# Four dense layers with their operands as scaled pairs of float16 instead of float32r, in longer phases

## The chip, the core and the metric

The kernel runs on one core of a Trainium2 chip. The metric is device time in microseconds (us) of one execution. Engines of the core that matter here: TensorE (PE in the profile, its weight loads PEld), VectorE (DVE), ScalarE (ACT), GpSimd (POOL) and SyncE (SP), which issues nearly all DMAs. Each engine works through its own queue in order.

## What is computed

An attention with a soft cap over 2 batches, 12 heads, 448 rows and 64 columns a head, then two dense pairs of layers on the 896 x 768 result:

```python
scores = cap * np.tanh(scale * np.matmul(q, k.transpose(0, 1, 3, 2)) / cap)
attn = softmax(scores)                     # sum + 1e-9 below the line
x = np.matmul(attn, v)                     # 896 tokens x 768
h = x @ w_in;  g = np.maximum(h, 0.0) ** 2 # 768 -> 2048
x = g @ w_out                              # 2048 -> 768
h = x @ w_in2; g = h / (1 + np.exp(-h))
out = g @ w_out2
```

The weights arrive as 64-bit floats; the kernel's own units turn them into 32-bit words first.

## The kernel before

**Attention** (`attention_bounded`, lines 413 to 583). Twelve pairs of heads (i = 0 to 11), two half steps each. For a half step PE makes the scores (L440), ACT takes tanh (L448) and exp (L451), DVE adds two exp tiles into a `half` tile (L469, L471), PE makes `px` = exp times v (L459) and, with a tile of ones, the row sums (L479). All these matmuls are in float32. DVE copies `px` into the cell `x_c{i}` (L490) and the sums into `sm` (L494); after every second pair the sums go through DRAM, where DVE inverts them (L508, L509) and a DMA spreads them into `rb` (L517). DVE multiplies the cell by `rb` (L522), and `Forms.now` lets POOL split the cell into a high part (L1031) and a low part (L1032) for the first dense layer. Cells 10 and 11 are divided without the detour (L529 to L531): their reciprocals are 128 x 448 and lie on DVE after everything else of the attention.

**Dense layers** a, b, c, d (`feed_forward`, lines 667 to 974). Every operand is split in two parts, high = the value in float32r, low = value minus high; a product is high*high + high*low + low*high, so three matmuls of K = 128. Weight tiles: ACT takes the head of the 64-bit float (L209), DVE shifts and joins it (L216) into the word `u`, ACT writes the high part (L237), DVE the low part (L248). Layers a and c work on pairs of inner tiles f, f+1 (2048 / 128 = 16 tiles): `Pair.plain` with 72 matmuls of 448 columns for (a,0), (a,2), (c,0), and else a scheme with seven products instead of eight, 63 matmuls, which needs sums and differences of the operands (`Pair.whole`, L262 and L1070 build them). The results are activated on ACT and split into `g` tiles (`parts`, L675). Layers b and d (`out_units`) multiply `g` with the second weights: 12 units of 448 columns (b) and 14 of 384 columns (d).

**Phases.** The 16 inner tiles go in four phases of four: two pairs of layer a, then the 12 units of b over these four tiles, and so on; after each phase but the first the new sums are added to `y` on DVE (L662) or written out by ACT. The same holds for c and d.

**Order.** All of it is laid out in Python before anything runs: `Stream` keeps a clock of its own for ACT, DVE and POOL with priced steps, and `chunk` puts background steps (weights, forms, splits) into the gaps in order of due time. PE's order is fixed by the program. Five weight slots `hl`, three raw tiles, four words `u`.

**End.** All engines load `cap` into a register after the first phase (L905); where its size is above 50 a second program (`attention_general` and the layers once more, names ending in g) runs after the first. In this case it doesn't.

In names of the profile a number of a buffer is left out: `ha_0f` is h of layer a, batch 0, for either tile of the pair; `x0f` holds the parts of the cells; a final f marks the first program.

## Time and profile before

| | |
|---|---|
| three runs | 549.84 us median, 549.43 to 553.88 |
| the profiled execution | 549.33 us |
| its span, first to last instruction | 547.4 us |
| PE busy | 539.6 us (99%) |
| DVE busy / ACT busy / POOL busy | 364.3 / 355.6 / 31.1 us |

The profiled execution is 1.9 us longer than its span. A busy PE is not PE at its peak, since matmuls overlap; pace is read from the time that a run of matmuls takes, divided by their number. "Idle before" in square brackets is the wait of that engine just before the instruction, with what ended it.

### The profile page before, as it was taken

The numbers are of one execution on the slowest core, as the hardware profiler recorded it, in microseconds if no ns is written. First come the engines' busy times: TensorE is split into PE (matmuls) and PEld (weight loads), VectorE is DVE, ScalarE is ACT, GpSimd is POOL, SyncE is SP. The second block draws the span as 40 slices with busy tenths as digits, with TensorE's granted clock in tenths as the row PEclk, the third lists the DMA queues.
The fourth block names the chain that finished last, engine by engine and source line by source line (L and its number), as shares of the span: only waits on it lengthen the run. The fifth ranks groups of instructions, "written<-read, shape, count | busy, mean of one in ns | idle before, by whom it ended". The sixth has DMA issues, their size and how long they took to land.

```text
span 547.4 us, 7123 instructions
## 1 busy us (share of the span) xinstructions
PE 539.6 (99%) x2739; PEld 452.6 (83%) x2739; DVE 364.3 (67%) x525; ACT 355.6 (65%) x533; POOL 31.1 (6%) x27
## 2 busy tenths in 40 slices
PE   8999999999999999999999999999999999999995
PEld 4333333899999999999999999999999999999995
DVE  0779987896755667566756997654686568656621
ACT  6999998388668626862688797756762486238400
POOL 1004444200000000000000000000000000000000
PEclk9999999999999999999999999999999999999999
DMA  8365552152331353135313331633351335130022
GB/s 224 128 178 163 171 180 85 58 186 103 116 116 59 115 174 115 59 116 173 116 59 115 116 116 58 223 124 116 116 174 59 115 113 176 59 115 1 23 108 77
DMA packets 18300, 64.25 MB, mean 117 GB/s; under 512 B 2578, under 2 KB 8722, under 8 KB 18258
## 3 DMA queue, kind: packets, MB, share of 16 engines
q1 hardware_dynamic: 18224, 63.72, 35.7%
q8 instruction: 23, 0.38, 0.3%
q14 instruction: 19, 0.16, 0.1%
q0 software_dynamic: 32, 0.00, 0.0%
q10 hardware_dynamic: 2, 0.00, 0.0%
HBM read 60.88 MB, written 2.79 MB: 116 GB/s over the span
## 4 chain that ended last, share of the span: by engine, by line
PE 97%; DMA 1%; SPq 0%; DVE 0%; issue 0%
PE px L459 7%; PE s L440 7%; PE yb_1f L686 4%; PE yb_4f L686 4%; PE yb_2f L686 4%; PE yb_0f L686 4%; PE yb_3f L686 4%; PE yb_5f L686 4%; PE yd_0f L956 3%; PE yd_6f L956 3%; PE yd_1f L956 3%; PE yd_3f L956 3%; PE yd_5f L956 3%; PE yd_4f L956 3%; PE yd_2f L956 3%; PE ha_0f L686 3%
## 5 line engine op out<-in xcount | busy, mean ns | idle before, releaser
L448 ACT ACTIVATE e<-s 112x896 f32<-112x896 f32 x48 | 41.7, 933 | 7.1 <-PE s L440 7.1
L451 ACT ACTIVATE e<-e 112x896 f32<-112x896 f32 x48 | 43.5, 975 | 0.0
L469 DVE TENSOR_TENSOR half<-e,e 112x896 f32<-112x896 f32 x24 | 27.4, 1147 | 2.9 <-ACT e L451 2.9
L471 DVE TENSOR_TENSOR half<-half,half 112x896 f32<-112x896 f32 x11 | 14.8, 1349 | 0.4
L494 DVE COPY sm<-sum 128x448 f32<-128x448 f32 x10 | 6.2, 621 | 8.8 <-PE sum L479 8.8
L479 PE MATMUL sum<-half,ones 112*64 112x448 f32 x52 | 11.9, 541 | 0.0
L662 DVE TENSOR_TENSOR x1f<-yaf,x1f 128x448 fp32r<-128x448 f32 x15 | 9.2, 621 | 1.4 <-ACT x1f L658 1.2
L662 DVE TENSOR_TENSOR ycf<-yd_6f,ycf 128x384 f32<-128x384 f32 x6 | 3.3, 558 | 9.1 <-PE yd_6f L956 9.1
L658 ACT ACTIVATE x1f<-yaf 128x448 fp32r<-128x448 f32 x15 | 8.4, 570 | 0.9 <-DVE yaf L662 0.8
L479 PEld LDWEIGHTS sum<-half,ones 112*64 112x64 f32 x52 | 3.6, 137 | 6.2 <-issue 4.9
L662 DVE TENSOR_TENSOR ycf<-yd_0f,ycf 128x384 f32<-128x384 f32 x6 | 3.3, 558 | 7.9 <-PE yd_0f L956 7.9
L662 DVE TENSOR_TENSOR yaf<-yaf 128x448 f32<-128x448 f32 x12 | 7.2, 622 | 0.5 <-ACT yaf L658 0.3
L662 DVE TENSOR_TENSOR ycf<-yd_5f,ycf 128x384 f32<-128x384 f32 x6 | 3.3, 558 | 5.7 <-PE yd_5f L956 5.7
L662 DVE TENSOR_TENSOR ycf<-yd_4f,ycf 128x384 f32<-128x384 f32 x6 | 3.3, 558 | 4.4 <-PE yd_4f L956 4.4
L662 DVE TENSOR_TENSOR ycf<-yd_1f,ycf 128x384 f32<-128x384 f32 x6 | 3.3, 558 | 4.2 <-PE yd_1f L956 4.1
L530 DVE RECIPROCAL r<-r 128x448 f32<-128x448 f32 x2 | 5.9, 2953 | 0.1
L237 ACT ACTIVATE hl_58f<-u_59f 128x768 fp32r<-128x768 f32 x1 | 0.8, 847 | 7.8 <-PE yd_6f L956 7.8
L237 ACT ACTIVATE hl_68f<-u_69f 128x768 fp32r<-128x768 f32 x1 | 0.8, 847 | 7.8 <-PE yd_6f L956 7.8
L209 ACT ACTIVATE zeros<-raw_wa9f 128x768 f16<-128x768 bf16 x1 | 1.1, 1087 | 7.1 <-DVE u_18f L216 7.1
L209 ACT ACTIVATE zeros<-raw_wa13f 128x768 f16<-128x768 bf16 x1 | 1.1, 1083 | 7.1 <-DVE u_28f L216 7.1
L662 DVE TENSOR_TENSOR ycf<-yd_3f,ycf 128x384 f32<-128x384 f32 x6 | 3.3, 558 | 3.4 <-PE yd_3f L956 3.3
L662 DVE TENSOR_TENSOR yaf<-yb_5f,yaf 128x448 f32<-128x448 f32 x4 | 2.5, 625 | 4.6 <-PE yb_5f L686 4.6
(2232 smaller groups left out, 1872.7 us busy)
## 6 DMA issues: line engine op xcount, KB each, us to landing
out<-ycf SPq DMA_DIRECT2D x14, 192.0 KB
rb<-scratch SPq DMA_DIRECT2D x10, 224.0 KB
raw_wb_0f<-in_moe_w_out SPq DMA_DIRECT2D x2, 768.0 KB
raw_wb_1f<-in_moe_w_out SPq DMA_DIRECT2D x2, 768.0 KB
raw_wb_2f<-in_moe_w_out SPq DMA_DIRECT2D x2, 768.0 KB
raw_wb_3f<-in_moe_w_out SPq DMA_DIRECT2D x2, 768.0 KB
raw_wb_4f<-in_moe_w_out SPq DMA_DIRECT2D x2, 768.0 KB
raw_wb_5f<-in_moe_w_out SPq DMA_DIRECT2D x2, 768.0 KB
```

The lines of the kernel that those rows point to most:

```text
L440: nc.tensor.matmul(sp[:CP, j, :S], lhsT=pr.qk[i][p, 1, c * CP : (c + 1) * CP], rhs=pr.qk[i][p, 0], start=True, stop=True,)
L448: nc.scalar.activation(t, sp[:CP, :, :S], AF.Tanh, scale=scale_s)
L451: nc.scalar.activation(ex[i, c], ex[i, c], AF.Exp, scale=scale_c)
L459: nc.tensor.matmul(px[i][64 * j : 64 * j + 64, :S], lhsT=pr.vt[i][:, j, c], rhs=ex[i, c][:, j], start=(c == 0), stop=(c == NC - 1),)
L469: nc.vector.tensor_tensor(t, ex[i, 2 * g], ex[i, 2 * g + 1], op=ALU.add)
L471: nc.vector.tensor_tensor(t, t, half[i, 0], op=ALU.add)
L479: nc.tensor.matmul(sums[i][64 * j : 64 * j + 64, :S], lhsT=ones[:CP], rhs=t[:, j], start=(n == 0), stop=(n == len(parts) - 1),)
L494: nc.vector.tensor_copy(t, sums.pop(i)[:, :S])
L658: return Step("A", cols, lambda: nc.scalar.activation(at(out), at(src), func), list(deps))
L662: return Step(eng, cols, lambda: e.tensor_tensor(at(out), at(x), at(y), op=op), list(deps))
L686: nc.tensor.matmul(acc, lhsT=w(e_w, kk), rhs=x(e_x, kk), start=first and i == 0, stop=last and i == len(n) - 1, skip_group_check=more,)
L956: nc.tensor.matmul(acc[:, :NW], lhsT=g[KD * e + kk][:, e_g, t * 128 : t * 128 + 128], rhs=hl[:, e_w, kk * NW : kk * NW + NW], start=first ...
```

## The change

The bounded program `f` gets its dense operands as float16 pairs: each operand is multiplied by a power of two (`POWER`) before it is split, and the results are scaled back in ACT's `scale` or in DVE's scalar operand. Tiles of the same bytes hold twice as many values, so there are ten weight slots instead of five. The general program keeps float32r and its four phases of four; both are written by the same code with another type and another plan.

In float16 PE gets a weight load and a matmul as two instructions for each product, where in float32r one instruction stands. The products are the same in number and shape: 1611 of 448 columns and 672 of 384 columns in the dense layers.

The phases of `f` are 4, 6 and 6 inner tiles in layers a and b, and 8 and 8 in c and d. The results of b are written once and added twice (before: three times), those of d written once and added once.

A watch is added: the low parts of all operands but the b weights and layer a's `g` are made with an accumulator output (`accum_out`, 144 instructions), 22 samples of high parts are squared and summed (`look` on DVE for cells 0 to 9, `sample` on ACT for twelve others), and at the end DVE judges them (`judge`), PE adds the 22 columns up over the partitions (L239 of the new kernel), and every engine loads the verdict `ok` (L1106) ten units into the last 14 units. The second program runs where `ok` is not 1.0; the register of `cap` is gone.

The planner looks six steps ahead in the background queues (`AHEAD`) instead of one, and may move a high part or a square from ACT to DVE (`either`). Counted in `f`: steps of 448 columns on DVE outside the attention 187 before, 202 now; sums of 384 columns 42 and 14; steps of 448 columns on ACT 265 and 246. DMAs carry the same bytes.

```diff
+    POWER = {"x0": 16, "a": 13, "b": 14, "ga": 22, "x1": 23, "c": 13, "d": 14, "gc": 24}
+    LOWS, SAMPLES = 224, NP2 + 10
+    LEAST = 256.0 * 128 * S
+    ONE = 2.0 ** -POWER["x0"]
...
+    COL2, COL4 = 0.1892, 0.1625
+    PROD, UNIT = 9 * COL2, 12 * COL2
...
+    plans = {"f": Plan((4,6,6),(8,8)), "g": Plan((4, 4, 4, 4), (4, 4, 4, 4))}
...
+    def low_part(watch, lo, x, hi, scale, see=True):
+        if watch is None:
+            nc.vector.tensor_tensor(lo, x, hi.bitcast(F32), op=ALU.subtract)
+        else:
+            nc.vector.scalar_tensor_tensor(
+                lo, x, scale, hi, op0=ALU.mult, op1=ALU.subtract, accum_out=watch.low() if see else None
+            )
...
+        def low(self):
+            self.n += 1
+            return self.lows[:, self.n - 1 : self.n]
...
+        def look(self, x):
+            self.m += 1
+            nc.vector.scalar_tensor_tensor(
+                self.junk, x, 1.0, x, op0=ALU.mult, op1=ALU.mult, accum_out=self.squares[:, self.m : self.m + 1]
+            )
...
+        def judge(self, capt):
+            assert self.n <= LOWS and self.m == SAMPLES
+            s, w = self.squares, self.within
+            nc.vector.tensor_scalar(self.signs[:, 0:1], capt[:1], CAP_MAX, None, op0=ALU.is_le)
+            nc.vector.tensor_scalar(self.signs[:, 1:2], capt[:1], -CAP_MAX, None, op0=ALU.is_ge)
...
+        def add_up(self, ones, acc):
+            nc.tensor.matmul(acc[:D, : 1 + SAMPLES], lhsT=ones, rhs=self.squares, start=True, stop=True)
...
+            self.nslots, self.nwords, self.nraw = (10, 4, 3) if watch else (5, 4, 3)
...
-                self.hl[i] = wpool.tile([128, 2, WT], F32R, tag="hl", bufs=SLOTS, name=f"hl_{j}{self.tag}")
+                self.hl[i] = self.wpool.tile([128, 2, WT], self.dt, tag="hl", bufs=self.nslots, name=f"hl_{j}{self.tag}")
...
+            b = Step("D", cols + 95 * (self.watch is not None and see), lambda: low_part(
+                self.watch, self.hl[key][:, 1], u(), self.hl[key][:, 0], scale, see
+            ), [a])
...
-                    able = [x for x in self.late if x.eng == eng and self.open(x, t)]
-                    if self.bg[eng] and self.open(self.bg[eng][0], t) and t + self.bg[eng][0].cost < self.now + 0.3:
-                        able.append(self.bg[eng][0])
+                    able = [
+                        x for x in self.late
+                        if (x.eng == eng or x.other and x.other.eng == eng and self.clock[x.eng] > t + SLACK)
+                        and self.open(x, t, eng)
+                    ]
+                    able += [
+                        x for x in self.bg[eng][:AHEAD] if self.open(x, t, eng) and t + x.cost < self.now + 0.3
...
-                nc.vector.tensor_scalar(gcap, gcap, 1e-9, None, op0=ALU.mult)
+                nc.vector.tensor_scalar(gcap, gcap, 1e-9 * ONE, None, op0=ALU.mult)
...
+    def high(out, src, scale, deps):
+        st = act(AF.Copy, out, src, deps, scale=scale)
+        return st.either(Step("D", S // 2, lambda: nc.vector.tensor_scalar(
+            at(out), at(src), scale, 1.0, op0=ALU.mult, op1=ALU.mult
+        )))
...
-        def gtile(f, name):
-            return gpool.tile([128, 2, B * S], F32R, tag=f"g{f % FP}", name=f"g{name}{f}{tag}")
+        def gtile(f, name, f0):
+            return gpool.tile([128, 2, B * S], dt, tag=f"g{(f - f0) % ws.todo.most}", name=f"g{name}{f}{tag}")
...
-            if ph == 0 and tag == "f":
-                capbits.append(
-                    nc.values_load(capt[0:1].bitcast(I32), min_val=-(2**31), max_val=2**31 - 1)
-                )
...
+        def judge():
+            ws.finish()
+            watch.judge(capt)
+        def add_up():
+            watch.add_up(ones[0], bank("judge"))
+        def read():
+            verdict.append(nc.values_load(watch.ok.bitcast(I32), min_val=0, max_val=0x3F800000))
...
+                    st = Step("D", NW, lambda: nc.vector.scalar_tensor_tensor(
+                        yb, acc, to_y, yb, op0=ALU.mult, op1=ALU.add
...
+            between = {units2[4]: judge, units2[7]: add_up, units2[10]: read} if watch and ph == len(phases["c"]) - 1 else {}
...
         def now(self, i):
@@ -1029,7 +1205,9 @@
             j, q = divmod(i, 4)
             (hi, lo), r = (self.form(self.OWN[q], j, e) for e in range(2)), self.cell(i)
             nc.gpsimd.tensor_scalar(hi, r, 1.0, 1.0, op0=ALU.mult, op1=ALU.mult)
-            nc.gpsimd.tensor_tensor(lo, r, hi.bitcast(F32), op=ALU.subtract)
+            if self.ws.watch:
+                self.ws.watch.look(hi)
+            nc.gpsimd.tensor_tensor(lo, r, hi.bitcast(F32) if self.dt == F32R else hi, op=ALU.subtract)
...
+            if self.ws.watch and i not in self.given and (self.y is None or i < 2):
+                p = self.OWN[q]
+                c = self.seen[i] = self.ws.watch.sample(lambda: self.form(p, j, 0), parts(p))
...
-    run(attention_bounded, "f")
-    (bits,) = capbits
-    with tc.If((bits & 0x7FFFFFFF) > CAP_MAX_BITS):
-        run(attention_general, "g")
+                scale = 2.0 ** (power["x1"] - power["ga"] - power["b"])
+                return Forms(ws, xtile("x1"), rest, y, plan.starts[1], sum(w == "c" for w, f in PLAIN), dt, scale)
+            feed_forward(ws, x0, x1_of, ytile, gpool, qpool, tag, dt, power, ones)
+    ones = []
+    run(attention_bounded, "f", F16)
+    (good,) = verdict
+    with tc.If(good < 0x3F800000):
+        run(attention_general, "g", F32R)
```

The order changes at two places of the attention's end. First DVE's queue in the attention, around the multiplication of cell 2 (`x_c2f`) by `rb`. Before:

```order
L469 TENSOR_TENSOR half_0_519<-e_0_485,e_1_490 112x896
L494 COPY sm_529<-sum_526 128x448
L522 TENSOR_TENSOR x_c2f<-x_c2f,rb_476 128x448
L239 TENSOR_SCALAR hl_1f<-u_1f 128x768
L469 TENSOR_TENSOR half_1_554<-e_2_506,e_3_511 112x896
L471 TENSOR_TENSOR half_1_554<-half_1_554,half_0_519 112x896
```

Of the change, the same place:

```order
L582 TENSOR_TENSOR half_0_528<-e_0_494,e_1_499 112x896
L607 COPY sm_538<-sum_535 128x448
L635 TENSOR_TENSOR x_c2f<-x_c2f,rb_485 128x448
L222 SCALAR_TENSOR_TENSOR junk,squares<-x0f 128x448
L342 TENSOR_SCALAR hl_1f<-u_1f 128x768
L582 TENSOR_TENSOR half_1_564<-e_2_515,e_3_520 112x896
L584 TENSOR_TENSOR half_1_564<-half_1_564,half_0_528 112x896
```

L222 is new; `squares` is a column of the watch, `junk` its unused product. It reads the high part that POOL makes from the product just before it, and it stands ahead of the `half` tiles; the same stands behind each of the ten multiplications.

Then DVE's queue from the last `half` tile on, where the last cells are finished and the first dense layer begins. Before:

```order
L469 TENSOR_TENSOR half_1_824<-e_2_798,e_3_803 112x896
L522 TENSOR_TENSOR x_c8f<-x_c8f,rb_821 128x448
L522 TENSOR_TENSOR x_c9f<-x_c9f,rb_821 128x448
L529 TENSOR_SCALAR r_842<-sum_808,gcap 128x448
L530 RECIPROCAL r_842<-r_842 128x448
L531 TENSOR_TENSOR x_c10f<-x_c10f,r_842 128x448
L529 TENSOR_SCALAR r_843<-sum_830,gcap 128x448
L530 RECIPROCAL r_843<-r_843 128x448
L662 TENSOR_TENSOR x0f<-x_c10f,x0f 128x448
L531 TENSOR_TENSOR x_c11f<-x_c11f,r_843 128x448
L248 TENSOR_TENSOR hl_2f<-u_2f,hl_2f 128x768
```

Of the change:

```order
L582 TENSOR_TENSOR half_1_839<-e_2_812,e_3_817 112x896
L635 TENSOR_TENSOR x_c8f<-x_c8f,rb_836 128x448
L222 SCALAR_TENSOR_TENSOR junk,squares<-x0f 128x448
L635 TENSOR_TENSOR x_c9f<-x_c9f,rb_836 128x448
L222 SCALAR_TENSOR_TENSOR junk,squares<-x0f 128x448
L642 TENSOR_SCALAR r_859<-sum_822,gcap 128x448
L643 RECIPROCAL r_859<-r_859 128x448
L644 TENSOR_TENSOR x_c10f<-x_c10f,r_859 128x448
L642 TENSOR_SCALAR r_860<-sum_845,gcap 128x448
L643 RECIPROCAL r_860<-r_860 128x448
L191 SCALAR_TENSOR_TENSOR x0f,lows<-x_c10f,x0f 128x448
L644 TENSOR_TENSOR x_c11f<-x_c11f,r_860 128x448
```

Two more reads of POOL's high parts now stand ahead of the two reciprocals, and the low part of cell 10 carries an accumulator.

## Rows read from the trace of the kernel before

**Rows 1.** The page's head: span, and busy us with its share, instructions.

```profile
span 547.4 us, 7123 instructions
PE 539.6 (99%) x2739; PEld 452.6 (83%) x2739; DVE 364.3 (67%) x525; ACT 355.6 (65%) x533; POOL 31.1 (6%) x27
```

**Rows 2.** Stages: us, busy us of each engine (instructions), granted clock, DMA share, GB/s.

```profile
0.00:96.43 96.43, 94.94 (x457) 33.62 (x457) 69.06 (x88) 86.77 (x107) 27.35 (x23) 1.00 0.53 162
96.43:541.16 444.73, 444.71 (x2283) 419.03 (x2283) 294.66 (x436) 268.87 (x427) 3.71 (x4) 1.00 0.33 109
96.43:125.81 29.38, 29.38 (x145) 27.25 (x146) 27.72 (x37) 18.49 (x31) 3.71 (x4) 1.00 0.37 128
319.15:346.30 27.15, 27.15 (x136) 25.17 (x135) 22.33 (x36) 23.22 (x39) 0.00 (x0) 1.00 0.33 111
512.00:541.20 29.20, 29.14 (x169) 28.82 (x167) 9.51 (x18) 1.16 (x3) 0.00 (x0) 1.00 0.24 89
```

**Rows 3.** The chain that ended last: start us, us, what; layers a, b, d, c.

```profile
106.35 2.44 PE ha_0f L686 x12
...
135.54 2.43 PE yb_4f L686 x12
...
354.86 2.08 PE yd_4f L956 x12
...
394.25 1.86 PE cc6f L686 x9
```

**Rows 4.** The 16-bit warm-up of line 84: duration ns min/median/max, first and last start us.

```profile
L84 PEld LDWEIGHTS <-idle x20: 103/151/151, 1.1 to 4.9; 128*128 128x128 bf16 x20
L84 PE MATMUL idle<-idle x20: 394/421/422, 1.1 to 5.1; 128*128 128x256 bf16 x20
```

**Rows 5.** Attention in stretches of 7.5 us, columns as in the stages.

```profile
45.00:52.50 7.50, 7.50 (x38) 2.52 (x36) 7.43 (x10) 7.50 (x10) 2.30 (x3) 1.00 0.27 87
52.50:60.00 7.50, 7.50 (x40) 2.56 (x38) 6.80 (x9) 6.85 (x9) 4.56 (x3) 1.00 0.66 167
...
sum 51.40, PE 51.40 PEld 17.46 DVE 44.33 ACT 47.44 POOL 23.28; mean PE 7.34 PEld 2.49 DVE 6.33 ACT 6.78 POOL 3.33
```

**Rows 6.** DVE in order of time in the attention: start us, us, instruction.

```profile
35.71 1.09 DVE L471 TENSOR_TENSOR half<-half,half 112x896 f32<-112x896 f32 x1
...
49.80 0.60 DVE L522 TENSOR_TENSOR x_c1f<-x_c1f,rb 128x448 f32<-128x448 f32 x1
50.33 1.07 DVE L469 TENSOR_TENSOR half<-e,e 112x896 f32<-112x896 f32 x1
...
59.28 1.92 DVE L471 TENSOR_TENSOR half<-half,half 112x896 f32<-112x896 f32 x1
```

**Rows 7.** POOL's high and low parts in order of time.

```profile
50.49 1.34 POOL L1031 TENSOR_SCALAR x0f<-x_c1f 128x448 fp32r<-128x448 f32 x1 [5.12 <-DVE x_c1f L522]
...
98.77 1.16 POOL L1032 TENSOR_TENSOR x0f<-x_c8f,x0f 128x448 fp32r<-128x448 f32 x1
99.90 0.56 POOL L1031 TENSOR_SCALAR x0f<-x_c9f 128x448 fp32r<-128x448 f32 x1
```

**Rows 8.** DVE in order of time, end of the attention and first dense layer.

```profile
97.11 0.63 DVE L522 TENSOR_TENSOR x_c8f<-x_c8f,rb 128x448 f32<-128x448 f32 x1 [2.27 <-DMA rb<-scratch]
97.65 0.62 DVE L522 TENSOR_TENSOR x_c9f<-x_c9f,rb 128x448 f32<-128x448 f32 x1
98.18 0.68 DVE L529 TENSOR_SCALAR r<-sum,gcap 128x448 f32<-128x448 f32 x1
98.89 2.95 DVE L530 RECIPROCAL r<-r 128x448 f32<-128x448 f32 x1
...
106.01 0.56 DVE L662 TENSOR_TENSOR x0f<-x_c10f,x0f 128x448 fp32r<-128x448 f32 x1
...
108.95 0.96 DVE L216 SCALAR_TENSOR_TENSOR u_4f<-raw_wb_0f,zeros 128x768 int32<-128x768 int32 x1
109.82 0.96 DVE L248 TENSOR_TENSOR hl_3f<-u_3f,hl_3f 128x768 fp32r<-128x768 f32 x1
```

**Rows 9.** Small or 384-column instructions of DVE, and one register load of PE.

```profile
L547 DVE TENSOR_SCALAR gcap<-capt 128x1 f32<-128x1 f32 x1 | 0.2, 154 | 4.2 <-DMA capt<-in_cap 4.2
L662 DVE TENSOR_TENSOR ycf<-yd_6f,ycf 128x384 f32<-128x384 f32 x6 | 3.3, 558 | 9.1 <-PE yd_6f L956 9.1
L905 PEldq TENSOR_LOAD <-capt x1: 490/490/490, 122.0 to 122.0; - x1
```

More of the change, by code (lines that the diff above doesn't have):

```diff
@@ L23 @@
 CAP_MAX = 50.0
-CAP_MAX_BITS = 0x42480000
 @with_exitstack
@@ L77, in bank2 @@
         return spool.tile([128, 2, 512], F32, tag="s", bufs=2, name=name)
-    idle = work.tile([128, S], F32, tag="r", bufs=7, name="idle")
+    idle = work.tile([128, S], F32, tag="r", bufs=NR, name="idle")
     nc.vector.memset(idle[:, :128], 0.0)
@@ L154, in __init__, with either, change @@
             self.cost = fix + col * cols
-            self.end = self.due = None
+            self.end = self.due = self.other = None
+        def either(self, other):
+            self.other = other
+            return self
+        def change(self):
+            o = self.other
+            self.eng, self.fn, self.cost, self.other = o.eng, o.fn, o.cost, None
+    def low_part(watch, lo, x, hi, scale, see=True):
[5 more added lines that the diff above has]
+            )
@@ L195, in is_free, with room @@
                 return None
-            return -1.0 if n < SLOTS else self.freed.get(self.slots[n - SLOTS])
+            return -1.0 if n < self.nslots else self.freed.get(self.slots[n - self.nslots])
+        def room(self):
+            n = len(self.words)
+            return -1.0 if n < self.nwords else self.read[self.words[n - self.nwords]].end
         def turn_steps(self, i):
@@ L308, in begin @@
             self.loading = True
-            self.load_to(sum(d.end is not None for d in self.turned) - 1 + RAW)
+            self.load_to(sum(d.end is not None for d in self.turned) - 1 + self.nraw)
             for st in self.steps:
@@ L332, in run_first, with open @@
                 self.run(q.pop(0))
-        def open(self, st, now):
-            if any(d.end is None or d.end + (HOP if d.eng != st.eng else 0) > now for d in st.deps):
+        def open(self, st, now, eng):
+            if any(d.end is None or d.end + (HOP if d.eng != eng else 0) > now for d in st.deps):
                 return False
@@ L842, in run_pairs, with out_units @@
             for f in fs[::2]:
+                if watch and f == 0:
+                    watch_later(ws.get(ws.todo.where[w, f])[:, 0, :S])
                 p = Pair(w, f, x, g, done, funcs)
                 (p.plain if (w, f) in PLAIN else p.first if f == 0 else p.whole)()
-        def out_units(w, ph, units, unit, us, end, seed=None):
-            e0 = FP // KD * ph
+        def out_units(w, ph, units, unit, us, end, seed=None, between={}):
+            e0, e1 = (f // KD for f in ws.todo.phases[w][ph])
             accs, seeds = {}, {}
@@ L878, in out_units @@
             head, tail = units[:4], units[4:]
-            for e in range(e0, e0 + FP // KD):
+            for e in range(e0, e1):
                 for n, u in head:
@@ L882, in out_units @@
             for n, u in tail:
-                for e in range(e0, e0 + FP // KD):
+                for e in range(e0, e1):
                     go(n, u, e)
-        NPH = FT // FP
+                if (n, u) in between:
+                    between[n, u]()
+        phases = ws.todo.phases
         g, done = {}, {}
@@ L914, in unit1 @@
                     acc[:, :S], lambda ew, kk: hl[:, ew, kk * NW + m * 128 : kk * NW + m * 128 + 128],
-                    lambda ex, kk: half(g[KD * e + kk][:, ex], b), range(KD), first, last, ph == NPH - 1,
+                    lambda ex, kk: half(g[KD * e + kk][:, ex], b), range(KD), first, last, ph == len(phases["a"]) - 1,
                 )
```

339 lines of the change are left out of this document (216 added, 123 removed).

## The prediction

> **What bounds the kernel now.** I read the page's head first: PE is busy for 539.6 of 547.4 us, DVE and ACT for two thirds [rows 1]. Then the stages: the attention lasts to 96.43 us, the dense layers from there to 541.16, and in these 444.73 us PE is idle for 0.02 us at a granted clock of 1.00 [rows 2]. So the dense layers last as long as PE's stream of 2283 matmuls needs, and nothing else sets their end. The chain of waits gives the stream's pace: 12 matmuls of 448 columns in 2.43 us (202.7 ns each), 12 of 384 columns in 2.08 us (173.3 ns), and in the products of layer c 9 in 1.86 us (206.7 ns) [rows 3]. Check: 1170 x 0.2027 + 441 x 0.2067 + 672 x 0.1733 = 444.8 us, the stage's length. At 2.4 GHz, the upper of the clock's two levels, 448 columns at one column a cycle are 186.7 ns and 384 are 160.0. So float32r pays 8 to 11% on the bare columns.
>
> In the attention PE is busy too, but DVE is close behind: 7.43 of 7.50 us in one stretch, 6.80 in the next, 44.33 of 51.40 over the seven stretches [rows 5]. The first dense stage is tight on DVE as well, 27.72 of 29.38 us [rows 2].
>
> **Term 1: the stream in float16.** Number and shape of the products stay, the pace is what changes. The trace has no 16-bit matmul of 448 columns. Nearest row: the warm-up's 16-bit matmuls of 256 columns, with a weight load of their own each, start 4.0 us apart over 19 steps, 211 ns each, 0.82 ns a column [rows 4]. That is one column a cycle of the lower level (213 ns) with nothing on top, while the 151 ns of the loads lie beside the matmuls. The granted clock is printed as 1.00 there, which doesn't fit; so I take from it only that a 16-bit stream shows no surcharge. Bounds of the pace: bare columns from below (186.7 and 160.0), float32r's pace from above. I take 189 and 162, near the lower bound, by the warm-up, with 1% left because float32r's own streams differ by 2% between layers. New length: 1611 x 0.189 + 672 x 0.162 = 413.3 us, a gain of **31.4 us**; by the lower bound 408.3 and 36.4, by the upper none.
>
> The Trainium skill (TensorE: Matmul & The Clock Gate, section "Wait — 56ns, not 53.3ns?") states a fixed cost of about 2.5 ns per warm matmul on top of columns over 2.4 GHz. By that 189.2 and 162.5 ns, 414.0 us and a gain of 30.7. Float32r's rows don't agree with it (16 ns on top); no run here shows it for 16 bits.
>
> **Term 2: ten reads of POOL's work in DVE's queue.** In the attention every `look` (L222) stands right behind the product it depends on, so DVE now waits for POOL there, and behind it stand the `half` tiles that PE's sums need. One look costs: semaphore 0.09, POOL's high part 0.56 when DVE is quiet (1.34 under load), 0.08 back [rows 7], and the look itself, 448 columns like other DVE steps of two operands (0.60) plus its accumulator [rows 6]. The trace has no accumulator; from below it costs nothing, from above one more small instruction of 0.154 [rows 9]. I take 0.1. Together 1.42 us for each of the cells 0 to 7, 11.4 us. DVE's idle time in the seven stretches takes 51.40 - 44.33 = 7.1 of it [rows 5]. Some comes back: POOL's low part now lies beside the look and L469 and no longer beside L471, which takes 1.92 in that company and 1.09 alone [rows 6]; at 0.35 for each of eight, 2.8. Rest **1.5 us**, by which the last `half` tile, PE's last sums and the first dense matmul come later. Bounds: 0, and 8 x 2.2 - 7.1 = 10.5 with POOL at 1.34.
>
> **Term 3: the last cells.** Before, the products of cells 8 and 9 and the first step for cell 10 start at 97.11, 97.65 and 98.18, and the low part of cell 10 ends 8.4 us after the last, at 106.57 [rows 8]. PE's second part of the first pair begins at 106.35 [rows 3] and wants that low part with its fifth matmul, at 107.16: 0.6 us of slack. After: the `rb` data land about 1.0 later, since L508 and L509, which feed them, stand in the delayed queue: product at 98.1 to 98.7, POOL's high part to 99.36, look to 100.1, product of cell 9 to 100.65. POOL is then at the low part of cell 8 (1.16, to 100.6) and makes the next high part in 0.56 [rows 7], to 101.3; second look to 102.05. Plus 8.4 and 0.1 for the accumulator: 110.6. PE, which began at 97.93, gets there at 97.93 + 52 x 0.189 = 107.8. It stands for **2.9 us**. Bounds 0 (data earlier, slack elsewhere) and 6 (POOL at 1.34 twice, more lag).
>
> **Term 4: the weights of tile 3.** Their low part (L248, 109.82 before [rows 8]) now stands behind product, high and low part of cell 11, the low part of weight tile 2, a difference, a shift and four steps for `g`: 7.3 us behind 110.6, 117.9. PE wants it with the fifth matmul of the second tile of pair (a,2): 100.8 + 72 x 0.189 + 16 x 0.189 = 117.4. **0.6 us**; bounds 0 and 3.
>
> **What I cost at nothing.** DVE in the dense layers: 15 more steps of 448 columns and 144 accumulators at 0.1 against 28 fewer sums of 0.558 [rows 9]: 294.66 + 8 = about 303 of 418 us; ACT loses 19 steps. The cover is the quarter of the time in which either is idle; where it is thin (22.33 of 27.15 behind the change to layer c [rows 2]) the longer b phase ahead spaces the tiles of x further apart. Longer phases also give PE a later need for the last `g` tiles, and ten slots hold the weights of three pairs. The judging lies in the last units, where DVE is busy for 9.51 of 29.20 us [rows 2]. PE's load of the verdict is 0.49 us on its queue [rows 9], like the load that goes away, and three units (11.7 us) stand between PE's addition and it; without that cover DVE's three small steps and the load, about 1 us.
>
> **Sum.** The profiled execution has 549.33 us (span 547.4 [rows 1] and 1.9 around it). 549.33 - 31.4 + 1.5 + 2.9 + 0.6 = 522.9; the median of the runs is 0.5 above that execution: **523.4 us**.
>
> **The rivals.**
>
> *The late cells are hidden.* If DVE's waits fall into its idle time and the `rb` data come no later, terms 2 to 4 vanish: 549.84 - 31.4 = 518.4. For it: 7.1 us of idle DVE. Against: 0.6 us of slack at cell 10. Chance 0.12.
>
> *DVE becomes the bound in the dense layers.* An accumulating step could run through its elements twice, since DVE has to stream two operands and to add up. Price: the element time of the rows again, 0.47 us for 448 columns, 0.81 for 768, 0.40 for 384 (each row less 0.154 [rows 8, 9]); for the 70, 61 and 13 accumulating low parts 87 us, DVE at about 380 of 413. In the stage behind the change to layer c some 40 us of DVE work would meet 25 of PE, 15 us late, and 5 to 10 more in the first dense stage: about 543. Smaller overloads of the same stages give 530 to 537. For it: the tight stages. Against: the shift (L216), a step of the same kind on two 32-bit operands without accumulator, takes 0.96, as much as L248 [rows 8]. The Trainium skill (Vector Engine (DVE) Microarchitecture Reference, section "7. Points that are easy to get wrong") states this halving for two sources in SBUF that aren't bf16; L216 does not show it, and no run here has the accumulator. Chance 0.08 for the full price, 0.06 for the smaller ones.
>
> *The stream doesn't gain (the other side).* If two instructions for each product, or the operands' path, hold PE at float32r's pace, term 1 is gone and the delays stay: 549.84 + 5.0 = 554.8, slower. It decides at a gain below 5.0 us, a pace of 448 columns above 200.5 ns, and each ns more is 2.3 us. Against it: the warm-up. Chance 0.05.
>
> *The verdict fails.* If a scaled operand left float16's range, the second program would follow the branch: at least a second 444.7 us of dense layers [rows 2], above 960. Against: x0 is about 0.005 in size and scaled by 65536, the weights are 0.02 to 0.04 and scaled by 8192 and 16384, all in the hundreds. Chance 0.02.
>
> **How the numbers follow.** The forecast itself has 0.67; with the bounds of the pace and delays of 3 to 9 us it spans 517 to 529. The range 515 to 533 leaves out the doubled DVE work, the last two rivals, and the far ends, less than 2 in 10. A measurement of this kernel can tell about 1%, so faster means below 544.3: 0.67 + 0.12 + most of 0.14 = 0.91. Within 1%: 0.05. Slower by over 1% (above 555.3): a pace above 203 ns or the second program, 0.04.
>
> **What would show it.** Term 1: in the chain after, 12 units of 448 columns in 2.27 us and of 384 in 1.95; 2.43 would make it wrong. Term 2: DVE waiting for POOL at L222, 0.6 to 1 us each, and the first dense matmul at 97 to 99. Term 3: an idle PE of about 3 us near 108, released by DVE's low part of cell 10; if the granted clock falls to the lower level behind it, every us there costs half a us more. The DVE rival: 448-column L191 at 1.1 us in place of 0.7, and PE waiting for L191 between 330 and 345. The forecast fails above all if the dense layers show idle PE elsewhere than in their first 25 us.

## The result and the profile after

| | before | after |
|---|---|---|
| median of the runs | 549.63 us (4 runs, 549.04 to 553.88) | 529.19 us (4 runs, 528.02 to 530.77) |
| the profiled execution, its span | 549.33, 547.4 us | 529.49, 527.7 us |

The ratio is 0.9614, with a 95% interval of 0.956 to 0.9669: faster by 20.4 us. The forecast was 523.4, so the kernel is 5.8 us slower than forecast, inside the range of 515 to 533.

The head of the page after, in answer to [rows 1] (span; busy us of each engine with its share and instructions):

```profile
span 527.7 us, 7255 instructions
...
PE 512.7 (97%) x2741; PEld 256.5 (49%) x2741; DVE 363.5 (69%) x687; ACT 345.1 (65%) x526; POOL 22.4 (4%) x28
```

PE has 15 us without work now where it had 7.8. The chain that ended last gives the pace, as in [rows 3] (start us, us, what; layers b, b, a, d, c):

```profile
142.55 2.28 PE yb_4f L829 x12
...
210.81 3.40 PE yb_4f L829 x18
...
238.05 1.70 PE aa10f L829 x9
...
379.64 3.90 PE yd_4f L1126 x24
...
418.64 1.70 PE ac8f L829 x9
```

That is 189.2 ns for 448 columns (eight units of 18 matmuls from 210.81 to 238.05) and 162.5 for 384 (ten units of 24 from 379.64 to 418.64); the products of layers a and c have the same pace, 1.70 us for 9. The whole stream takes 1611 x 0.1892 + 672 x 0.1625 = 414.0 us against 444.7 before: 30.7 us less. The span fell by 19.7 only. Where the other 11 us went is in what PE waited for (us in total, times, longest):

```profile
PE ha_0f L829 <- DVE x0f L191: 3.1, 1, 3.1
PE sum L592 <- DVE half L584: 2.4, 4, 0.9
```

and in the order of time on PE around the start of the dense layers (start us, us, instruction, idle time before and what ended it):

```profile
100.04 0.97 PE L592 MATMUL sum<-half,ones 112*64 112x448 f32 x4 [1.10 <-DVE half L582]
100.95 2.44 PE L829 MATMUL ha_0f<-x0f,hl_0f 128*128 128x448 f16 x12
...
110.04 1.07 PE L829 MATMUL ha_0f<-x0f,hl_0f 128*128 128x448 f16 x4
114.22 0.54 PE L829 MATMUL ha_0f<-x0f,hl_0f 128*128 128x448 f16 x2 [3.11 <-DVE x0f L191]
```

The dense layers begin at 100.95 instead of 96.36 (the stages of [rows 2] are cut 0.07 us behind that start). After 52 matmuls the stream stops for DVE's low part of cell 10. Behind that stop the granted clock is lower for a while (windows, columns as in [rows 2]):

```profile
110.00:115.00 5.00, 1.89 (x11) 0.80 (x9) 4.93 (x7) 1.45 (x4) 0.00 (x0) 1.00 0.00 0
115.00:120.00 5.00, 5.00 (x19) 2.23 (x18) 4.26 (x10) 3.05 (x7) 0.00 (x0) 0.66 0.17 32
```

The chain has the matmuls of that stretch,

```profile
114.22 2.40 PE ha_0f L829 x8
116.62 3.23 PE ha_1f L829 x12
```

20 in 5.63 us, at full pace 3.78.

What makes both late stands on DVE, in order of time:

```profile
96.23 0.60 DVE L635 TENSOR_TENSOR x_c7f<-x_c7f,rb 128x448 f32<-128x448 f32 x1
97.52 0.63 DVE L222 SCALAR_TENSOR_TENSOR junk<-x0f 128x448 bf16<-128x448 f16 x1 [0.69 <-POOL x0f L1207]
98.07 0.08 DVE L222 DVE_READ_ACCUMULATOR junk<-x0f 128x1 f32 x1
98.07 1.92 DVE L582 TENSOR_TENSOR half<-e,e 112x896 f32<-112x896 f32 x1
101.22 0.63 DVE L635 TENSOR_TENSOR x_c8f<-x_c8f,rb 128x448 f32<-128x448 f32 x1 [1.23 <-DMA rb<-scratch]
102.53 0.62 DVE L222 SCALAR_TENSOR_TENSOR junk<-x0f 128x448 bf16<-128x448 f16 x1 [0.69 <-POOL x0f L1207]
...
103.09 1.45 DVE L635 TENSOR_TENSOR x_c9f<-x_c9f,rb 128x448 f32<-128x448 f32 x1
105.22 0.63 DVE L222 SCALAR_TENSOR_TENSOR junk<-x0f 128x448 bf16<-128x448 f16 x1 [0.69 <-POOL x0f L1207]
...
106.49 2.95 DVE L643 RECIPROCAL r<-r 128x448 f32<-128x448 f32 x1
...
113.60 0.56 DVE L191 SCALAR_TENSOR_TENSOR x0f<-x_c10f,x0f 128x448 f16<-128x448 f32 x1
```

and on POOL:

```profile
97.57 1.47 POOL L1210 TENSOR_TENSOR x0f<-x_c7f,x0f 128x448 f16<-128x448 f32 x1
```

Each look waits 0.69 us for POOL and works 0.63; the reading of its accumulator, 0.08, starts together with the next operation (both at 98.07) and doesn't hold it up. The operation behind a look lies beside POOL's low part and is stretched: the half sum (L582) takes 1.92 there, the product of cell 9 takes 1.45.

The accounts of the span, before to after: stream -30.7, dense start +4.6, stop at cell 10 +3.4 (PE would have gone on at 110.04 + 4 x 0.189 = 110.8), lower clock +1.85, small waits in the later dense layers (0.7 of it for the weights `hl_7` in the first units of b) and the end +1.1. Sum -19.75; measured -19.7.

### The profile page after: what moved, and what is told of

The parts are those of the page before. It is cut to its first block, busy times and chain, and to the rows that moved or that the text cites. A ratio compares the mean times of both kernels' runs of the same rounds, so it can differ in the third digit from the quotient of the medians.

```text
span 527.7 us, 7255 instructions
## 1 busy us (share of the span) xinstructions
PE 512.7 (97%) x2741; PEld 256.5 (49%) x2741; DVE 363.5 (69%) x687; ACT 345.1 (65%) x526; POOL 22.4 (4%) x28
## 4 chain that ended last, share of the span: by engine, by line
PE 83%; DVE 10%; ACT 2%; DMA 2%; issue 1%; POOL 1%; SPq 0%; DVEq 0%
PE yb_4f L829 3%; PE yb_3f L829 3%; PE yb_1f L829 3%; PE yb_2f L829 3%; PE yb_0f L829 3%; PE yb_5f L829 3%; PE yd_1f L1126 3%; PE yd_6f L1126 3%; PE yd_0f L1126 3%; PE yd_5f L1126 3%; PE yd_4f L1126 3%; PE yd_3f L1126 3%; PE yd_2f L1126 3%; DVE half L582 3%; PE s L553 3%; PE px L572 2%
## 5 line engine op out<-in xcount | busy, mean ns | idle before, releaser
L582 DVE TENSOR_TENSOR half<-e,e 112x896 f32<-112x896 f32 x24 | 30.9, 1290 | 2.0 <-ACT e L564 2.0
L584 DVE TENSOR_TENSOR half<-half,half 112x896 f32<-112x896 f32 x11 | 12.0, 1092 | 0.4
L222 DVE SCALAR_TENSOR_TENSOR junk<-x0f 128x448 bf16<-128x448 f16 x10 | 6.3, 626 | 6.9 <-POOL x0f L1207 6.9
L191 DVE SCALAR_TENSOR_TENSOR x1f<-yaf,x1f 128x448 f16<-128x448 f32 x15 | 9.1, 622 | 2.8 <-ACT x1f L770 2.7
L770 ACT ACTIVATE ha_0f<-ha_0f 128x448 f32<-128x448 f32 x7 | 3.9, 557 | 6.1 <-PE ha_0f L829 6.0
L829 PEld LDWEIGHTS <-hl_0f 128*128 128x128 f16 x36 | 3.8, 107 | 8.0 <-issue 5.6
L829 PE MATMUL ha_0f<-x0f,hl_0f 128*128 128x448 f16 x18 | 4.0, 352 | 3.1 <-DVE x0f L191 3.1
L770 ACT ACTIVATE x1f<-yaf 128x448 f16<-128x448 f32 x11 | 6.3, 571 | 0.8 <-DVE yaf L781 0.6
L191 DVE SCALAR_TENSOR_TENSOR hl_63f<-u_63f,hl_63f 128x768 f16<-128x768 f32 x1 | 1.0, 959 | 7.2 <-ACT hl_63f L340 7.2
L829 PEld LDWEIGHTS <-hl_1f 128*128 128x128 f16 x36 | 3.7, 102 | 3.7 <-issue 0.7
L93 PE MATMUL idle<-idle 128*128 128x256 bf16 x20 | 4.4, 420 | 1.1 <-DVE idle L90 1.1
```

The source lines that it names most:

```text
L191: nc.vector.scalar_tensor_tensor(lo, x, scale, hi, op0=ALU.mult, op1=ALU.subtract, accum_out=watch.low() if see else None)
L582: nc.vector.tensor_tensor(t, ex[i, 2 * g], ex[i, 2 * g + 1], op=ALU.add)
L584: nc.vector.tensor_tensor(t, t, half[i, 0], op=ALU.add)
L770: return Step("A", cols, lambda: nc.scalar.activation(at(out), at(src), func, scale=scale), list(deps))
L829: nc.tensor.matmul(acc, lhsT=w(e_w, kk), rhs=x(e_x, kk), start=first and i == 0, stop=last and i == len(n) - 1, skip_group_check=more,)
```

## The experiments

The theory to test: the ten looks cost by their place in DVE's queue, twice, as a late start of the dense layers and as the stop at cell 10 with the clock behind it. The rivals: the loss comes with float16 itself (accumulators, 16-bit operands on DVE or POOL), or the looks cost by their work wherever they stand.

One number serves all runs: the time from the first product of cell 0 on DVE to the first dense matmul on PE. The first of these is where the looks begin, and runs differ by up to 2.6 us ahead of it (41.63 to 44.27), where no look stands yet. The two rows of before (DVE, then PE) and of the changed kernel:

```profile
41.92 0.61 DVE L522 TENSOR_TENSOR x_c0f<-x_c0f,rb 128x448 f32<-128x448 f32 x1
...
96.36 1.89 PE L686 MATMUL ha_0f<-x0f,hl_0f 128*128 128x448 f32 x8
```

```profile
41.67 0.62 DVE L635 TENSOR_TENSOR x_c0f<-x_c0f,rb 128x448 f32<-128x448 f32 x1
```

| kernel | median us (lowest to highest) | cell 0 to dense start | PE's wait for cell 10 |
|---|---|---|---|
| before | 549.63 (549.04 to 553.88) | 54.44 | 0 |
| the change | 529.19 (528.02 to 530.77) | 59.28 | 3.11 |
| no look | 520.23 (520.08 to 520.37) | 54.44 | 0.75 |
| look later | 520.70 (519.95 to 520.98) | 54.44 | 0.58 |
| only the last two later | 524.53 (524.14 to 525.57) | 59.29 | 0 |
| fillers | 527.86 (526.93 to 529.04) | 59.27 | filled |
| before, with looks | 559.16 (557.07 to 560.00) | 60.04 | 2.22 |
| phases of four | 530.23 (529.76 to 531.77) | 59.27 | 2.90 |
| no accumulators | 529.19 (528.09 to 529.51) | 59.24 | 3.10 |
| early reciprocal | 520.66 (520.46 to 521.11) | 54.44 | 0, cell 11 0.35 |
| later still | 521.14 (520.83 to 521.91) | 54.44 | 1.53 |
| one cell behind | 524.52 (523.96 to 526.34) | 54.47 | 3.11 |

**No look.**

```diff
-    LOWS, SAMPLES = 224, NP2 + 10
+    LOWS, SAMPLES = 224, NP2
...
             nc.gpsimd.tensor_scalar(hi, r, 1.0, 1.0, op0=ALU.mult, op1=ALU.mult)
-            if self.ws.watch:
-                self.ws.watch.look(hi)
```

> The changed kernel without the ten reads (look) of POOL's high parts on DVE; it leaves out the range test of cells 0 to 9, and the verdict goes by the other samples. Theory A, the looks cause the late start of the dense layers, the stall at cell 10 and the fallen clock behind it: the first dense matmul comes back from 100.95 to 96.4 to 97, no idle time of PE at cell 10, granted clock 1.00 there, and 529.2 - 4.3 - 3.4 - 1.85 = 519.6 us (518.5 to 521). Theory B, they come from the rest of the float16 form (accumulators of the low parts, DVE's operations on 16-bit operands, the clock by itself): 527 to 529.5 us, and at most the 0.7 us of each of the last two reads gone. It also shows what DVE's next half sum (L582) costs beside POOL without a look: 1.9 us if POOL's own two operations slow it, 1.07 if only the order behind a look does.

Theory A holds: 520.23, ratio to before 0.9463 (0.9411 to 0.9515). The start of the dense layers is back to the hundredth, and the clock is 1.00 throughout the dense layers. A wait of 0.75 is left at cell 10, so that much of the stop isn't the looks': counted from cell 0, PE comes there 0.95 us earlier than in the kernel before, and the `rb` data for cells 8 and 9 reach DVE 0.5 later. DVE's half sums take nearly as long in sum without the looks as with them (groups: count | busy us, mean ns | idle before; the kernel before, the changed one, this one):

```profile
L469 DVE TENSOR_TENSOR half<-e,e 112x896 f32<-112x896 f32 x24 | 27.4, 1147 | 2.9 <-ACT e L451 2.9
L471 DVE TENSOR_TENSOR half<-half,half 112x896 f32<-112x896 f32 x11 | 14.8, 1349 | 0.4
```

```profile
L582 DVE TENSOR_TENSOR half<-e,e 112x896 f32<-112x896 f32 x24 | 30.9, 1290 | 2.0 <-ACT e L564 2.0
L584 DVE TENSOR_TENSOR half<-half,half 112x896 f32<-112x896 f32 x11 | 12.0, 1092 | 0.4
```

```profile
L582 DVE TENSOR_TENSOR half<-e,e 112x896 f32<-112x896 f32 x24 | 27.2, 1137 | 1.8 <-ACT e L564 1.8
L584 DVE TENSOR_TENSOR half<-half,half 112x896 f32<-112x896 f32 x11 | 14.6, 1331 | 0.4
```

42.2, 42.9 and 41.8 us: POOL stretches whichever of them lies beside it, and the looks mainly moved that from L584 to L582.

**Look later.** Each look stands behind the half sums of the next half step (`flush` issues the pending ones), those of cells 8 and 9 in `late`, behind the reciprocals.

```diff
-                self.ws.watch.look(hi)
+                self.pending.append(hi)
...
                 add(last, (h - 1) % 2)
+                x0.flush()
...
+            for hi in self.pending:
+                st = Step("D", S + 95, lambda hi=hi: self.ws.watch.look(hi))
+                st.due = self.ws.now + 40.0
+                self.ws.later(st)
```

> The same ten looks, but each stands behind the two half sums of the next half step instead of right behind its product, and those of the last two cells are due 40 us into the dense layers; no work is left out. Theory A1, the place is what costs (DVE waits 0.69 us for POOL ten times, and the last two stand ahead of the reciprocals): first dense matmul at 96.5 to 97.5, no stall at cell 10, 519 to 521 us. Theory A2, the looks' own 0.7 us costs wherever it stands in the attention, since DVE is too full there: first dense matmul at 98.5 to 100, no stall at cell 10, 522 to 524 us. Theory B, other work: 527 to 529.5 us.

A1: the same ten looks, all of the work, and the dense layers start as in the kernel before. DVE takes the looks into its idle time:

```profile
L222 DVE SCALAR_TENSOR_TENSOR junk<-x0f 128x448 bf16<-128x448 f16 x10 | 6.1, 614 | 0.1
```

0.1 us of waiting for all ten, 6.9 in the changed kernel. The ratio to before is 0.9472 (0.942 to 0.9524). This version leaves nothing out and beats both kernels, the changed one by 8.5 us of the medians; the intervals of the two ratios don't meet.

**Only the last two later**: cells 8 and 9 as in the run above, the other eight as in the change.

```diff
-            if self.ws.watch:
-                self.ws.watch.look(hi)
+            if self.ws.watch and i in (8, 9):
+                self.pending.append(hi)
+            elif self.ws.watch:
+                self.ws.watch.look(hi)
```

> Only the looks of cells 8 and 9 go into the dense layers, the other eight stay where the change has them; no work is left out. Theory A: the first dense matmul stays at about 100.9 (the eight looks in the attention still delay it), cell 10's low part comes 3.3 us earlier (at 110.9 instead of 114.2), PE's idle time there falls from 3.11 to under 0.3 and the clock doesn't fall: 529.2 - 3.3 - 1.85 = 524.0 us (523 to 525.5). If the looks of 8 and 9 aren't the cause of the stall (cell 10 is late by the sum or by the reciprocals): stall over 2 us, 527 to 529.5 us.

As theory A had it: the late start stays whole (59.29), the stop at cell 10 is gone (0.40 us of waiting for the weights `hl_3` come in its place), the clock is 1.00, and 4.7 us are won. So the two effects are separate: eight looks make the late start, two make the stop.

**Fillers.**

```diff
+                            if last and (self.w, self.f, b, ff) == ("a", 0, 0, 0):
+                                fill = bank("fill")
+                                for _ in range(16):
+                                    nc.tensor.matmul(
+                                        fill[:, :S], lhsT=hl[:, 0, :128], rhs=self.x.form("p1", 0, 0), start=True, stop=True
+                                    )
```

> The changed kernel with 16 matmuls of 448 columns (3.0 us at 189 ns) into an unused bank put where PE waits for cell 10; nothing is left out, and the stall itself stays. If the idle time is what lowers the granted clock behind it: the 20 matmuls after the wait take 3.8 us instead of 5.6, and 529.2 - 1.85 = 527.3 us. If the clock falls by itself at that place (or those matmuls wait for something else): 529.2 us, and 5.6 us for the 20. If the fillers themselves come late and stretch the wait: up to 531 us.

```profile
110.36 3.19 PE L977 MATMUL fill<-x0f,hl_0f 128*128 128x448 f16 x16
113.39 1.45 PE L829 MATMUL ha_0f<-x0f,hl_0f 128*128 128x448 f16 x6
```

```profile
115.00:120.00 5.00, 5.00 (x29) 2.57 (x27) 4.93 (x11) 4.27 (x9) 0.00 (x0) 1.00 0.13 34
```

With PE busy through the wait the clock stays at 1.00 (0.66 without) and the matmuls behind it run at full pace: from the first dense matmul to the end of this pair PE takes 16.8 us, 18.7 without the fillers. The profile shows the 1.85 us; the medians differ by 1.3, about what the runs of either kernel scatter, so they alone would not settle it.

**Before, with looks**: the ten looks in the kernel before, at the place of the change. Their unused product goes into cell 11, which ACT fills behind the last look; PE has no wait for that.

```diff
             nc.gpsimd.tensor_scalar(hi, r, 1.0, 1.0, op0=ALU.mult, op1=ALU.mult)
+            if self.ws.tag == "f":
+                nc.vector.scalar_tensor_tensor(
+                    self.cell(NP2 - 1), hi.bitcast(F32), 1.0, hi.bitcast(F32), op0=ALU.mult, op1=ALU.mult,
+                    accum_out=squares[:, i : i + 1]
+                )
```

> The kernel before (float32r) with only the ten looks added at the place where the change has them. Theory A, the look's place costs what it costs whatever the operands: first dense matmul at 100 to 101.5 instead of 96.4, a stall of PE at cell 10 of 1.5 to 3 us (float32r reaches that cell later than float16 does, by 52 matmuls of 17.5 ns, and has a little more room), together 549 + 4.3 + 2.3 = 555.6 us, 557.5 if the clock falls behind the stall too. Theory B, the loss needs float16's operands (POOL's or DVE's 16-bit writes): 549 to 551 us, first dense matmul before 98.

Float32r pays a price of the same kind: 559.16 us, ratio 1.0155 (1.0101 to 1.0209), slower by an interval that lies on both sides of 2%, with the waits of PE in the same places:

```profile
PE sum L480 <- DVE half L472: 3.1, 5, 1.0
PE ha_0f L687 <- DVE x0f L663: 2.2, 1, 2.2
```

I had expected 555.6 to 557.5. Of the 10.3 us more in the span of the profiled run 5.6 are the late start, 2.2 the stop, behind which the clock stayed at 1.00, and 2.35 lie ahead of cell 0, where no look stands. There PE waits for the first load, and the clock falls behind that wait:

```profile
10.59 3.25 PE L460 MATMUL px<-e,vt0f 112*64 112x448 f32 x8 [2.12 <-DMA vt0f<-in_v]
```

```profile
10.50:14.00 3.50, 3.41 (x10) 1.08 (x12) 1.27 (x3) 2.16 (x5) 0.00 (x0) 0.51 1.05 328
```

In the kernel before the same 8 matmuls start at 9.84 and take 1.72 us; so 0.75 of the 2.35 are the later load and 1.5 the lower clock.

**Phases of four.**

```diff
-    plans = {"f": Plan((4,6,6),(8,8)), "g": Plan((4, 4, 4, 4), (4, 4, 4, 4))}
+    plans = {"f": Plan((4, 4, 4, 4), (4, 4, 4, 4)), "g": Plan((4, 4, 4, 4), (4, 4, 4, 4))}
```

> The changed kernel with the phases of before (four of four inner tiles in both pairs of layers); nothing is left out. The prediction gave the phases no price: 529.2 us within 1, dense layers as long as in the changed kernel. If the longer phases do pay (fewer partial sums of y to add, fewer first units behind a weight), this is slower: 530.5 to 533 us. If they cost (more inner tiles to hold, later starts), it is faster: 526 to 528 us.

530.23 with runs that overlap those of the change: by the medians unclear. The profile has two waits that the change does not have,

```profile
PE yd_0f L1126 <- DVE hl_43f L191: 1.0, 1, 1.0
PE bc2f L829 <- DVE hl_41f L191: 0.7, 1, 0.7
```

so the longer phases are worth up to 1.7 us, for which the prediction had nothing. DVE is busy for 385.0 us here and for 363.5 in the change, so most of the work that the longer phases save was off PE's path. In this run PE's wait at cell 10 was 2.90 and the clock behind it stayed at 1.00.

**No accumulators.**

```diff
-                lo, x, scale, hi, op0=ALU.mult, op1=ALU.subtract, accum_out=watch.low() if see else None
+                lo, x, scale, hi, op0=ALU.mult, op1=ALU.subtract, accum_out=None
```

> The changed kernel without the accumulator of the low parts (L191), so that the watch on the low parts is left out; the looks keep theirs. Theory A, an accumulator costs 0.08 us of DVE each and none of them lies on the path but those by cell 10: 528.7 to 529.4 us, L191 as long as with the accumulator (0.62 us for 448 elements, 0.95 for 768). Theory B, an accumulator makes DVE run the elements at half pace: L191 falls to 0.4 us or less, DVE has some 30 us less to do, and the dense layers lose their small waits: 526 to 528 us.

The time is that of the change. L191 is as long with the accumulator (first row, the change) as without (second row):

```profile
L191 DVE SCALAR_TENSOR_TENSOR x1f<-yaf,x1f 128x448 f16<-128x448 f32 x15 | 9.1, 622 | 2.8 <-ACT x1f L770 2.7
L191 DVE DVE_READ_ACCUMULATOR x1f<-yaf,x1f 128x1 f32 x15 | 1.2, 82 | 0.0
```

```profile
L191 DVE SCALAR_TENSOR_TENSOR x1f<-yaf,x1f 128x448 f16<-128x448 f32 x15 | 9.1, 621 | 2.9 <-ACT x1f L770 2.8
```

An accumulator costs nothing of the element time, and its own read of 82 ns lies beside the operation behind it: with the 144 reads DVE is busy for 363.5 us, without them for 362.0.

**Early reciprocal**: look later, and in addition the first two steps of cell 10 (`early`: sum and reciprocal) ahead of the products of cells 8 and 9 (in `todo`), and a gate that keeps the looks of these two back

```diff
+        early = last_sums(i - 1)
+        for st in early[:2]:
+            st.fn()
+            st.end = 0.0
         for f, _ in todo:
             f()
...
-        x0.late(last_sums(i - 1), last_sums(i))
+        x0.late(early[2:], last_sums(i))
...
+                st.gate = lambda: 50.0
```

> e2 with two orders more: the reciprocal of cell 10's sums stands ahead of the products of cells 8 and 9 (DVE waits 1.74 us for their factors there in e2), and the looks of cells 8 and 9 don't start before 50 us into the dense layers; nothing is left out. If the two waits of PE that are left in e2's first dense layer (0.58 us for cell 10, 0.61 us for hl_3) are just that late: both gone, 520.7 - 1.2 = 519.5 us (518.8 to 520). If other work moves into their place (cell 11, or the products of cells 8 and 9 then late): a wait for x0 elsewhere in that layer, and 520 to 521.5 us.

The second case: both waits are gone and two others stand in their place, 520.66 us.

```profile
109.90 1.07 ACT L309 ACTIVATE zeros<-raw_wb_1f 128x768 f16<-128x768 bf16 x1 [1.01 <-DVE u_4f L316]
...
111.86 2.43 PE L834 MATMUL ha_0f<-x0f,hl_2f 128*128 128x448 f16 x12 [1.14 <-ACT ha_0f L775]
```

The two waits are 0.35 us for cell 11 and 1.14 for ACT. The 1.14 us come from ACT, which had a weight's head (L309) next in its queue and stood 1.01 us for DVE's word `u_4f` before it could activate `ha_0f`.

**Later still**: look later with that gate alone.

```diff
                 st.due = self.ws.now + 40.0
+                st.gate = lambda: 50.0
```

> e2 with one order more: the looks of cells 8 and 9 don't start before 50 us into the dense layers, so that hl_3's low part isn't behind them; nothing is left out. If they are what made PE wait 0.61 us for hl_3: that wait gone, the 0.58 us for cell 10 stays, 520.7 - 0.6 = 520.1 us (519.6 to 520.6). If hl_3 is late by other work: 520.7 us.

The wait for `hl_3` is gone, yet the time is not lower (521.14): in the profiled run DVE had the `rb` data 1.2 us later than in "look later" (first row, this kernel; second, "look later"; 0.9 counted from cell 0), and PE's wait for cell 10 was 1.53.

```profile
98.48 0.63 DVE L635 TENSOR_TENSOR x_c8f<-x_c8f,rb 128x448 f32<-128x448 f32 x1 [2.70 <-DMA rb<-scratch]
```

```profile
97.26 0.63 DVE L635 TENSOR_TENSOR x_c8f<-x_c8f,rb 128x448 f32<-128x448 f32 x1 [1.74 <-DMA rb<-scratch]
```

What is left at cell 10 follows the landing of these data, which differs between the two profiled runs by more than the gate gives: counted from cell 0 their DMA is issued at the same time, 51.0 us, and lands 0.9 apart. What sets that stays open.

**One cell behind**: each look stays at its place but reads the high part of the cell before, which POOL finished long ago. So none stands behind cell 0's product, and the tenth goes into the dense layers.

```diff
-                self.ws.watch.look(hi)
+                self.pending.append(hi)
+                if len(self.pending) > 1:
+                    self.ws.watch.look(self.pending.pop(0))
...
```

> The changed kernel with each look at its place, but reading the high part of the cell before (POOL has long written it), and the last one late in the first dense layer; the same number of looks, nothing left out. It takes away the wait of 0.69 us and keeps the look's 0.7 us of work at the same place of DVE's order. Theory wait: the first dense matmul at 96.2 to 97.5, the two looks that still stand between the last products and the reciprocals make cell 10 1.4 us later than in e2, so PE waits some 2.0 us there: 520.7 - 0.6 + 1.4 = 521.5 us (521 to 522.5, up to 1.8 more if the clock falls behind that wait). Theory place: the look delays the half sum behind it with or without a wait, first dense matmul at 99 to 101, 525 to 529 us.

This parts the wait from the work. With the work of seven of the eight looks at the same place and no wait the dense layers start as early as without looks (54.47): without the wait the late start is gone. Waits without the work were not run. The total of 524.52 is just above the 524.3 that theory wait had as its most, with the clock fallen, by the tail; counted from cell 0 the `rb` data reach DVE 0.8 us later than in "look later", and then:

```profile
99.42 0.97 DVE L635 TENSOR_TENSOR x_c9f<-x_c9f,rb 128x448 f32<-128x448 f32 x1
100.31 1.45 DVE L222 SCALAR_TENSOR_TENSOR junk<-x0f 128x448 bf16<-128x448 f16 x1
```

```profile
105.00:110.00 5.00, 1.70 (x9) 0.68 (x7) 4.93 (x5) 1.25 (x3) 0.00 (x0) 0.90 0.00 0
110.00:115.00 5.00, 4.86 (x14) 1.98 (x14) 4.56 (x11) 2.13 (x4) 0.00 (x0) 0.50 0.00 0
```

Beside POOL the second look takes 1.45 us instead of 0.62; PE stands for 0.33 and 3.11 us, and then the clock is at its lower level: 20 matmuls of 448 columns from 110.14 to 116.71, 2.8 us more than at full pace.

## Why the prediction was right, and where it was off

The direction and its cause were right; the 5.8 us too little are in the main one mis-sized term and one effect that it named and left out of the sum. Of its signs the paces, DVE's waits at L222 and PE's 3 us of idle time at cell 10 came true; the first dense matmul came at 100.95 and not at 97 to 99, and 0.7 us of idle PE lie behind the first 25 us of the dense layers.

**Term 1, the stream.** -31.4 forecast, -30.7 measured. The forecast took 189 and 162 ns by the warm-up rows [rows 4], of which it read that a 16-bit stream has no surcharge, and left 1% for another reason. But those rows have the pace of the lower level, and at the upper one the trace has 2.5 ns on top of the bare columns for both widths (189.2 - 186.7, 162.5 - 160.0). So the 1% was what hit, and that is luck in part. The new kernel's planner prices the same two matmuls at 0.1892 and 0.1625 us (`COL2`, `COL4`), which the prediction doesn't mention. The Trainium skill (TensorE: Matmul & The Clock Gate, section "Wait — 56ns, not 53.3ns?") gave 189.2 and 162.5, as an estimate from its 2.5 ns on top of columns over 2.4 GHz; the trace agrees to a tenth of a ns, for both widths.

**Term 2, the looks in the attention.** +1.5 forecast, +4.84 measured, 59.28 - 54.44. This is the step that failed, in two pieces of it: DVE's idle time and the relief. The windows from cell 0's product to the end of the last half sum show it (before, after):

```profile
41.92:94.84 52.92, 52.92 (x260) 18.01 (x258) 47.38 (x58) 48.82 (x59) 24.58 (x16) 1.00 0.47 145
```

```profile
41.67:99.99 58.32, 54.77 (x262) 17.62 (x258) 52.43 (x76) 49.62 (x60) 16.31 (x16) 1.00 0.45 139
```

The look's price was nearly right: 1.42 forecast, 1.31 measured, since the half sum behind a look starts 1.84 us after the product (98.07 - 96.23) and before started 0.53 after it [rows 6]; the accumulator, put at 0.1, costs next to nothing. The idle time was put too high: DVE has 5.5 us of it ahead of the last half sum (52.92 - 47.38), not 7.1, and gave 5.2. After, 5.9 us are idle, of which 5.5 are the eight waits for POOL and 0.4 are left. And the relief of 2.8 didn't come. L584 did lose what L471 had paid beside POOL (14.8 to 12.0 us for the 11), exactly the 2.8; but the operation that now follows the look pays instead, which the forecast did not charge: L582 rose from 27.4 (L469) to 30.9 us for the 24, and the high part of two weights (L342) from 0.55 to 1.39 each. Only the small L508 (L621) gave 1.8 back. Together these rows are +0.6 in place of -2.8, and +0.1 on DVE's time line, where the rows of neighbours overlap a little. So 8 x 1.31 - 5.2 + 0.1 = 5.4, the 58.32 - 52.92; 0.6 of it came back behind the last half sum, which the first dense matmul follows after 0.96 us instead of 1.52: 4.8. "One cell behind" shows that the work of seven looks fits into the idle time. Waits and work together overflow it; the waits alone, 5.5 us, would about fill it.

**Term 3, the last cells.** +2.9 forecast, +3.4 measured, by the mechanism forecast: product, POOL, look, product, POOL, look, reciprocal. All of it lay 3 us later than forecast, cell 10 and PE alike, because of term 2; the half us more is the product of cell 9 beside POOL (1.45 for 0.62). "Only the last two later" took it all away.

**Term 4, the weights of tile 3.** +0.6 forecast, nothing measured: the low part of `hl_3` ends at 121.8, and PE, which had started later, stopped and slowed down, wants it at 122.7. In "look later", where PE is hardly stopped, PE does wait 0.61 us for `hl_3`, by the two late looks ahead of it; "later still" has no such wait.

**The granted clock.** The forecast said that if the clock fell behind the stop each us there would cost half a us more, and put nothing into the sum: +1.85 in the profiled run, and "fillers" shows that the stop brings it.

**At nothing.** The judging, the load of the verdict and the accumulators cost PE 0.1 us at most, as forecast; the 144 accumulators, put at 0.1 us of DVE each, took 1.5 together. The phases, also at nothing, are worth up to 1.7 us, and 1.1 us of small waits in the later layers were not foreseen.

**The rivals.** DVE as the bound by accumulators that double the element time is refuted by "no accumulators". The Trainium skill (Vector Engine (DVE) Microarchitecture Reference, section "7. Points that are easy to get wrong") states that halving; the trace does not agree, for a float32 source with a float16 one (0.62 us for 448 columns with and without accumulator). "The late cells are hidden" (518.4) did not happen in the changed kernel; "look later" comes near it with 520.70, the difference being 0.6 us each for cell 10 and `hl_3`, 0.7 of the stream, and small waits. The stream gained, and the second program did not run.

## What to carry to other kernels

A read of another engine's fresh result belongs a few operations behind it in the queue, not right behind: in the attention the late start of 4.8 us was gone once the reads didn't wait for POOL, though seven of the eight still did their work at the same place, and two such reads ahead of the last serial chain cost 4.7 more, the lower clock behind them included. When a step moves and takes an operation out of the neighbourhood of another engine, charge the operation that comes into it; the stretching moved and did not go away. Behind a stop of PE read the granted clock before putting the matmuls there down as slow by themselves.

## What the runs showed of the hardware

- DVE and POOL stretch one another. Beside POOL's low part a half sum took 1.92 us instead of 1.07, a product of 448 columns 1.45 instead of 0.62, a 768-column high part 1.39 instead of 0.55, while the reciprocal (2.95) stayed the same beside POOL's parts of cells 8 and 9 [rows 7, 8]. POOL's high part took 0.57 in the change, where DVE waits for it, and up to 1.34 before. The Trainium skill (GPSIMD Engine Reference, section "1. Specifications") lists contention with DVE instructions that have two inputs in SBUF or run in a 2-port perf mode; the half sum and the product, with two inputs each, agree with it, and for the high part, with one, no run here shows the mode.
- The clock behind a stop was not the same from run to run: a mean of 0.66 in the window behind 3.11 us without matmuls (the change), 0.71 behind 3.10 ("no accumulators"), 0.50, the lower of its two levels (1.2 GHz) throughout, behind 0.33 and 3.11 ("one cell behind"), 0.51 behind 2.12 at the first load ("before, with looks"), but 1.00 behind 2.90 ("phases of four") and behind 2.22 at cell 10 ("before, with looks"). What parts these cases stays open here.
- A float16 product of 128 x 128 x 448 takes 189.2 ns at the upper level of the clock, with a separate weight load of 98 ns beside it; one of float32r took 202.7 to 206.7.
